# Other PSUM banks for the attention steps, and later places for one pair's V sums and for weight conversions

## The chip, the cores and the metric

The kernel runs on one core of a Trainium2 chip. The metric is the device time of one execution in microseconds. Before the change three runs took 580.83 us in the median (580.19 to 583.82).

Five engines work side by side, each with its own queue in order: TensorE (PE), VectorE (DVE), ScalarE (ACT), GpSimd (POOL) and SyncE (SP, which issues nearly all DMAs). PE writes its results to PSUM, which has eight banks of 2 KB in each of 128 partitions.

## The reference

Three layers follow each other, for a batch of 2, 768 positions and 8 heads of 64:

```
scores_l = scale * q @ k.T                      # only |i - j| < 16 counts
k_sum, v_sum = max of k, mean of v, over blocks of 32 positions
scores_s = scale * q @ k_sum.T + log(32)        # 24 block columns
a = softmax(concat(scores_l masked, scores_s))
x = a @ concat(v, v_sum)                        # attention, then heads side by side: 768 x 512

h = relu(x.T @ w_tok1) @ w_tok2                 # token mixing
u = x + h.T
x2 = u + relu(u @ w_ch1) @ w_ch2                # channel mixing, 512 -> 1536 -> 512

xn = layer_norm(x2) * g_ln
out = x2 + relu(xn @ w1) @ w2                   # 512 -> 2048 -> 512
```

## The kernel before, in words

**The attention part.** The heads are taken in pairs: two heads fill 128 partitions, and eight pairs, 0 to 7, make up both batches. A pair has twelve windows of 64 queries. A step handles four windows of a pair, so there are 24 steps, and step n belongs to pair n // 3. The keys of a window are 96 neighbours and the 24 block columns, 120 in all.

A step goes through six functions. `att_qk` (L378) makes the scores: 16 small matmuls into PSUM. `att_exp` (L398) has DVE add the mask and take the extreme of each row (L409, four instructions), and ACT take the exponential (L419, four instructions). `att_tr` (L421) transposes the four blocks of probabilities on PE into one bank of the pool `ps_pt`. `att_evac` (L429) has ACT copy that bank to SBUF (L433). `att_av` (L435) multiplies with V: 16 matmuls into one bank of the pool `ps_av`. `att_norm` (L454) has DVE divide by the row sums (L460, L463) into `u`.

**The preparation of a pair.** `prep_k` (L326, DVE) and `copy_k` (L339, ACT) make the block maxima of K. `prep_v1` (L345) makes the block sums of V: on DVE for pair 0, on POOL for the other pairs (L358, L361), from the transposed copy VT. `prep_v2` (L363) transposes these sums on PE (L367), into a bank of the same pool `ps_pt`, and ACT copies them into V in two instructions (L369). Q, K and V have three buffers each, VT and Z (the sums) two.

**PSUM banks.** The pool `ps_mm` has two banks for everything else. The scores are one tile of two banks: its axes are the window's parity j (one bank each), the step's parity, and the window couple. So two successive steps stand in two halves of the same two banks. `ps_pt` and `ps_av` have two banks each. Dependencies within a PSUM tile are kept bank by bank: an instruction of PE that writes a bank waits for the readers of that bank. A pool with n buffers hands a bank out again when all who used it are done.

**Weights.** The weights come as 64-bit words and are rebuilt as fp32 in halves of 512 columns. `conversion` (L160) is a generator of small pieces. For the first halves, four pieces make up one half: a load of a later half (`load_half`, L184, on SP, three buffers), one ACT instruction (L133) and three DVE instructions (L150, L152, L156), and the split into a rounded part (ACT, L203) and a rest (DVE, L228). During attention at most the first eight halves are done (L1107).

**Order of the work.** `attention` (L1019) writes out an order by hand: `put(at, ...)` enters a function at a place `at`, counted in steps, and the entries are sorted by place. PE keeps this order exactly. The other engines get theirs from a planner that goes by the same order and by its own estimate of when things are ready. The entries of step n are: scores at n, exponentials at n + 0.5, transposes at n + 1.1, the copy at n + 1.55, products at n + 2.15, and the normalisation at n + 2.6, with pieces of conversion woven in: `self.ops` pieces, which is 0 at the start, 4 from place 3.5 and 2 from place 8.58. Up to place 8.58 each step also has four matmuls on zeros, which keep PE busy (`fill`, L1070). The transpose of pair i's V sums stands at 3i - 0.2, ahead of the scores of step 3i at 3i and of the transposes of step 3i - 1 at 3i + 0.1; for pair 0 it stands at 1.6. From place 8.58 on, blocks of the token mixing are placed between the steps (`g1`, `g2`), and later the transposes for the channel mixing (`transpose_u`), at half steps or whole steps apart (L1049 to L1063).

**After attention** come the channel mixing, the layer norm and the last layer. PE's matmuls there run in an order set by loops in `run` (L1090).

Of the kernel before, what the change touches and what calls it, by code (L numbers as in the profile page):

```python
# [10 lines left out]
F32 = mybir.dt.float32  # L11
# [8 lines left out]
PSUM = bass.MemoryType.PSUM  # L20
DRAM = bass.MemoryType.DRAM

P = 128
# [37 lines left out]
class Kern:  # L61
# [316 lines left out]
    def att_qk(self, n):  # L378
        nc = self.nc
        i, qd = divmod(n, 3)  # L380
        Q, K = self.Q[i % 3], self.K[i % 3]
        ps = self.scores[:, :, n % 2]
        for e in range(2):
            for r in range(2):
                for j in range(2):
                    w = 4 * qd + 2 * e + j
                    a = 184 * (w // 2) + 88 * j
                    rows, cols = slice(64 * r, 64 * r + 64), slice(64 * (r ^ j), 64 * (r ^ j) + 64)
                    nc.tensor.matmul(  # L389
                        ps[cols, j, e, :NK],  # L390
                        Q[rows, 64 * w : 64 * w + 64],
                        K.rearrange("p v c -> p (v c)")[rows, a : a + NK],
                        start=True,
                        stop=True,
                    )
        self.sc[n] = ps
# [622 lines left out]
    def attention(self):  # L1019


        npair, nq = B * NPAIR, 3 * B * NPAIR
        O = ORDER
        ev = []
        put = lambda at, *fns: ev.append((at, len(ev), fns))
        for i in range(npair):
            at = 3 * i
            if i > 1:
                put(at + O["load_k"], lambda i=i: self.load_pair(i))
                put(at + O["load_vt"], lambda i=i: self.load_vt(i))  # L1030
                put(at + O["load_v"], lambda i=i: self.load_v(i))
            put(at + (O["kmax"] if i != 1 else -0.46), lambda i=i: self.prep_k(i))
            put(at + (O["copy_k"] if i != 1 else -0.44), lambda i=i: self.copy_k(i))
            put(at + O["vsum"] if i else O["vsum0"], lambda i=i: self.prep_v1(i))
            put(at + O["vput"] if i else O["vput0"], lambda i=i: self.prep_v2(i))
        for n in range(nq):
            put(n, lambda n=n: self.att_qk(n))
            if n < O["bg"]:
                put(n + 0.02, lambda: self.fill(2))
                put(n + 0.25, lambda: self.fill(2))  # L1040
            put(n + O["exp"], lambda n=n: self.att_exp(n))
            put(n + O["tr"], lambda n=n: self.att_tr(n))
            put(n + O["evac"], lambda n=n: self.att_evac(n))
            put(n + O["av"], lambda n=n: self.att_av(n))
            put(n + O["norm"], lambda n=n: self.weave(self.att_norm(n), self.convert(self.ops)))
        put(0.0, lambda: self.load_half(0), lambda: self.load_half(1))
        put(O["conv"], lambda: setattr(self, "ops", 4))
        put(O["bg"], lambda: setattr(self, "ops", 2))
        x0, x1, w0, w1 = self.g1(0, 0), self.g1(0, 1), self.g1(1, 0), self.g1(1, 1)  # L1049
        y, z0, z1 = self.g2(0), self.transpose_u(0), self.transpose_u(1)  # L1050
        low = {x0: 5 + O["lo"], x1: 11 + O["lo"], w0: 17 + O["lo"], w1: 23 + O["lo"]}
        need = {x0: 3, x1: 3, w0: 3, y: 6}
        pieces = [(x0, 0), (x0, 1), (x1, 0), (x1, 1)] + [(y, 1)] + [(y, 0.5)] * 5
        pieces += [(w0, 1), (w0, 0.5)] + [(z0, 0.5)] * 4 + [(z1, 0.5)] * 4 + [(w1, 0.5), (w1, 0.5)]
        at = O["bg"]
        for k, (g, gap) in enumerate(pieces):
            at += gap
            while at < low.get(g, 0):
                at += 0.5
            if g in need:  # L1060
                put(at, lambda g=g: self.convert_until(need[g]))
            put(at, lambda g=g: self.begin(g))
            put(at + O["fin"], lambda g=g: self.end(g))  # L1063
        for _, _, fns in sorted(ev, key=lambda e: e[:2]):
            for fn in fns:
                fn()
        while self.evacs:
            self.end(self.evacs[0])
# [21 lines left out]
    def run(self):  # L1090
        tc, nc, ctx = self.tc, self.nc, self.ctx
# [22 lines left out]
        xctx, actx = ExitStack(), ExitStack()  # L1114
# [1 line left out]
        self.att = actx.enter_context(tc.tile_pool(name="att", bufs=1, side="right"))  # L1116
        self.ps_mm = ctx.enter_context(tc.tile_pool(name="ps_mm", bufs=2, space=PSUM))
        ps_sc = actx.enter_context(tc.tile_pool(name="ps_sc", bufs=1, space=PSUM))
        self.scores = ps_sc.tile([P, 2, 2, 2, P], F32, name="scores")
        self.ps_pt = actx.enter_context(tc.tile_pool(name="ps_pt", bufs=2, space=PSUM))  # L1120
        self.ps_av = actx.enter_context(tc.tile_pool(name="ps_av", bufs=2, space=PSUM))

        att = self.att
        self.Q = [att.tile([P, S], F32, name=f"Q{i}") for i in range(3)]
# [67 lines left out]
        for n, (s, f, g) in enumerate(units):  # L1192
            if n == 0:
                order.enter_context(tc.manual_schedule(engines={mybir.EngineType.Activation}))
            c = 3 + f
# [28 lines left out]
            if xctx is not None and not self.bg and not self.evacs:  # L1224
# [7 lines left out]
                at = lambda f: self.slot(3 + f)  # L1232
# [130 lines left out]
```

## Time and profile before

| What | Value |
| --- | --- |
| Median of three runs | 580.83 us |
| Profiled execution | 580.95 us |
| Its span, first to last instruction | 579.2 us |
| PE busy | 561.1 us (97%) |
| DVE busy | 424.2 us (73%) |
| ACT busy | 296.8 us (51%) |
| POOL busy | 23.1 us (4%) |
| Mean granted clock of PE | 0.994 |

An engine is counted as busy while it executes, not while it waits. The shares are means over parts of the kernel with different limits, so the part that a change touches has to be read for itself. The granted clock is a share of PE's full speed: 1.00 is the level of 2.4 GHz, 0.50 that of 1.2 GHz.

### The profile page before, as it was taken

The page shows a single profiled execution, that of the slowest core. Times are in us where ns is not written, and L with a number is a line of the kernel's source. Part 1 is how long each engine was busy: PE and PEld are TensorE (multiplying, and loading weights), DVE is VectorE, ACT ScalarE, POOL GpSimd, SP SyncE. Part 2 cuts the span into 40 slices and gives each one's busy share as a digit, 9 for nine tenths or more (in the row PEclk, how much of TensorE's full clock was granted, in tenths as well). Part 3 has the DMA queues.
Part 4 walks back from the last instruction along what each step waited for, and adds up shares of the span by engine and source line. Part 5 has one row for each costly group of instructions (what it writes and reads, how often), then busy time and mean ns, then how long its engine had stood idle before and what let it go on. Part 6 is the DMA issues. An engine that isn't in the chain of part 4 may idle for free.

```text
span 579.2 us, 10262 instructions
## 1 busy us (share of the span) xinstructions
PE 561.1 (97%) x3651; PEld 494.7 (85%) x3656; DVE 424.2 (73%) x1012; ACT 296.8 (51%) x629; POOL 23.1 (4%) x54
## 2 busy tenths in 40 slices
PE   8798998999999999999999999999999999999997
PEld 3466776889998889999988988888898999999997
DVE  4598966576887689756659989686875986677781
ACT  4598757326875654755578455454331232233320
POOL 0424400000000000000000000000000000000000
PEclk9799999999999999999999999999999999999999
DMA  8999910133658766788936898786989998777545
GB/s 276 337 301 304 276 62 2 38 109 110 227 209 277 252 225 231 272 307 294 321 117 240 273 334 295 267 287 230 339 270 308 317 316 291 240 226 233 185 147 181
DMA packets 61417, 137.88 MB, mean 238 GB/s; under 512 B 5811, under 2 KB 19891, under 8 KB 61366
## 3 DMA queue, kind: packets, MB, share of 16 engines
q1 hardware_dynamic: 61360, 137.21, 71.8%
q8 instruction: 29, 0.48, 0.3%
q14 instruction: 22, 0.18, 0.1%
q10 hardware_dynamic: 6, 0.02, 0.0%
HBM read 102.60 MB, written 34.60 MB: 237 GB/s over the span
## 4 chain that ended last, share of the span: by engine, by line
PE 75%; DVE 10%; DMA 6%; ACT 5%; issue 2%; POOL 0%; SPq 0%; ACTq 0%; DVEq 0%; POOLq 0%
PE m L302 6%; PE m L304 5%; PE m L303 5%; PE acc_x L303 2%; PE acc_x L304 2%; PE acc_x L302 2%; PE g L475 2%; PE acc_y L304 2%; PE acc_y L303 2%; PE acc_y L302 2%; DMA VT<-in_vt_dram 1%; ACT pr L419 1%; PE av L446 1%; DMA w2s<-sp 1%; DMA wr<-w2s 1%
## 5 line engine op out<-in xcount | busy, mean ns | idle before, releaser
L302 PE MATMUL m<-slot,slot 128*128 128x384 f32 (+1 forms) x141 | 47.6, 338 | 1.9 <-DVE um L769 1.6
L304 PE MATMUL m<-slot,slot 128*128 128x384 f32 (+1 forms) x141 | 46.8, 332 | 0.0
L303 PE MATMUL m<-slot,slot 128*128 128x384 f32 (+1 forms) x141 | 46.8, 332 | 0.0
L303 PE MATMUL acc_x<-slot,ah 128*128 128x512 f32 x96 | 37.8, 394 | 0.0
L304 PE MATMUL acc_x<-slot,al 128*128 128x512 f32 x96 | 37.8, 394 | 0.0
L302 PE MATMUL acc_x<-slot,ah 128*128 128x512 f32 x96 | 37.5, 391 | 0.0
L419 ACT ACTIVATE pr<-sn,mn 128x120 f32<-128x120 f32 x96 | 30.2, 384 | 11.9 <-DVE mn L409 11.8
L302 PEld LDWEIGHTS m<-slot,slot 128*128 128x128 f32 x141 | 26.5, 188 | 5.4 <-DVE um L769 2.9
L303 PEld LDWEIGHTS m<-slot,slot 128*128 128x128 f32 x141 | 26.5, 188 | 1.5
L409 DVE CUSTOM_DVE_ANT_0 sn<-scores,mask 128x120 f32<-128x120 f32 x96 | 21.4, 277 | 8.3 <-PE scores L389 8.0
L304 PEld LDWEIGHTS m<-slot,slot 128*128 128x128 f32 x141 | 26.5, 188 | 0.0
L152 DVE SCALAR_TENSOR_TENSOR dec<-stage,dec 128x512 uint32<-128x512 uint32 x36 | 25.2, 700 | 0.5
L156 DVE SCALAR_TENSOR_TENSOR dec<-stage,dec 128x512 uint32<-128x512 uint32 x36 | 24.7, 687 | 0.4
L133 ACT ACTIVATE dec<-stage 128x512 f32<-128x512 f32 x36 | 24.2, 674 | 0.0
L760 ACT ACTIVATE ah<-sm 128x384 fp32r<-128x384 f32 x16 | 8.4, 526 | 30.7 <-DVE sm L769 30.7
L158 DVE SCALAR_TENSOR_TENSOR dec<-stage,dec 128x512 uint32<-128x512 uint32 x23 | 15.9, 690 | 9.5 <-ACT stage L139 9.3
L475 PE MATMUL g<-u,tok 128*128 128x256 f32 x96 | 22.5, 386 | 0.0
L304 PEld LDWEIGHTS acc_x<-slot,al 128*128 128x128 f32 x96 | 18.0, 188 | 4.0
L136 ACT ACTIVATE dec<-stage 128x512 f16<-128x512 f32 x23 | 18.4, 799 | 4.0 <-DMA stage<-in_wts_dram 4.0
L475 PEld LDWEIGHTS g<-u,tok 128*128 128x128 f32 x96 | 17.7, 190 | 2.9 <-issue 0.5
L358 POOL TENSOR_TENSOR VT<-VT 128x384 f32<-128x384 f32 (+3 forms) x28 | 18.3, 654 | 48.8 <-DMA VT<-in_vt_dram 47.1
L304 PE MATMUL acc_y<-slot,al_s 128*128 128x256 f32 x72 | 20.1, 280 | 0.0
(1492 smaller groups left out, 1760.1 us busy)
## 6 DMA issues: line engine op xcount, KB each, us to landing
stage<-in_wts_dram SPq DMA_DIRECT2D x62, 512.0 KB, 4.5
slot<-w1s SPq DMA_DIRECT2D x94, 256.0 KB, 4.1
w1s<-sps SPq DMA_DIRECT2D x16, 512.0 KB, 4.0
w2s<-sp SPq DMA_DIRECT2D x16, 512.0 KB, 3.0
slot<-w2s SPq DMA_DIRECT2D x16, 512.0 KB, 4.5
w2t<-wk SPq DMA_DIRECT2D x16, 512.0 KB, 4.7
slot<-w2t SPq DMA_DIRECT2D x8, 768.0 KB, 6.9
slot<-w2s SPq DMA_DIRECT2D x22, 256.0 KB, 4.3
```

Source lines behind the costliest of these rows:

```text
L133: nc.scalar.activation(m, high, AF.Abs, scale=2.0**-112)
L136: nc.scalar.activation(q[:, :, 1].bitcast(F16), high, AF.Copy, scale=2.0**-60)
L152: put(m, t[:, :, 1], 0x80000000, m, op0=ALU.bitwise_and, op1=ALU.bitwise_or)
L156: put(m, t[:, :, 0], 29, m, op0=ALU.logical_shift_right, op1=ALU.bitwise_or)
L158: put(m, t[:, :, 1], 3, m, op0=ALU.logical_shift_left, op1=ALU.bitwise_or)
L302: nc.tensor.matmul(out, lhs[0], rhs[0], start=first, stop=False)
L303: nc.tensor.matmul(out, lhs[0], rhs[1], start=False, stop=False)
L304: nc.tensor.matmul(out, lhs[1], rhs[0], start=False, stop=last)
L358: nc.gpsimd.tensor_tensor(cur[:, :, 0:n], cur[:, :, 0:n], cur[:, :, n : 2 * n], op=ALU.add)
L409: self.ttr[n] = nc.vector.tensor_tensor_reduce(sn[:, u], ps[:, u % 2, u // 2, :NK], self.mask[:, mv], scale=-SCALE, scalar=3e38, op0=ALU.a ...
L419: nc.scalar.activation(pr[:, u], sn[:, u], AF.Exp, bias=mn[:, u : u + 1], scale=-1.0)
L475: nc.tensor.matmul(ps[:, :256], self.tok1(st, t), self.u[:, b * ST + st, 256 * hf : 256 * hf + 256], start=st == 0, stop=st == ST - 1,)
```

## The change

- The scores become two tiles of two banks each. Step n uses tile n % 2; within it, window parity j still has a bank of its own. So the scores have four banks instead of two.
- `ps_pt` and `ps_av` get one bank each instead of two. All eight banks are in use before and after.
- The transpose of the V sums of pair 1, with its copies, moves from place 2.8 (3 - 0.2) to place 4.6 (3 + 1.6). Pair 0 and pairs 2 to 7 keep their places.
- `self.ops` is 0 from place 8.58, 4 from place 10.9 and 2 from place 16.9; before it was 2 from place 8.58 on.

```diff
@@ att_qk
-        ps = self.scores[:, :, n % 2]
+        ps = self.scores[n % 2][:, :, 0:256].rearrange("p j (e c) -> p j e c", e=2)
@@ attention
-            put(at + O["vput"] if i else O["vput0"], lambda i=i: self.prep_v2(i))
+            put(at + O["vput"] if i > 1 else at + O["vput0"], lambda i=i: self.prep_v2(i))
@@
-        put(O["bg"], lambda: setattr(self, "ops", 2))
+        for at, n in ((O["bg"], 0), (10.9, 4), (16.9, 2)):
+            put(at, lambda n=n: setattr(self, "ops", n))
@@ run
-        self.scores = ps_sc.tile([P, 2, 2, 2, P], F32, name="scores")
-        self.ps_pt = actx.enter_context(tc.tile_pool(name="ps_pt", bufs=2, space=PSUM))
-        self.ps_av = actx.enter_context(tc.tile_pool(name="ps_av", bufs=2, space=PSUM))
+        self.scores = [ps_sc.tile([P, 2, 512], F32, name=f"scores{i}") for i in range(2)]
+        self.ps_pt = actx.enter_context(tc.tile_pool(name="ps_pt", bufs=1, space=PSUM))
+        self.ps_av = actx.enter_context(tc.tile_pool(name="ps_av", bufs=1, space=PSUM))
```

## Rows read from the trace of the kernel before

**Rows 1.** Part 2 of the page: DMA share in 40 slices, in tenths.
```profile
DMA  8999910133658766788936898786989998777545
```
**Rows 2.** Table of stretches: length, busy us (instructions) per engine, clock, DMA, GB/s.
```profile
18.00:24.00 6.00, 5.25 (x52) 3.28 (x57) 3.12 (x13) 4.59 (x9) 0.36 (x2) 0.52 1.07 344
...
28.00:56.00 28.00, 25.47 (x355) 18.04 (x361) 25.01 (x114) 25.88 (x63) 9.55 (x18) 1.00 1.04 303
56.00:88.00 32.00, 31.95 (x334) 24.83 (x325) 23.99 (x94) 20.04 (x52) 6.58 (x13) 1.00 0.58 174
88.00:101.00 13.00, 11.23 (x173) 8.55 (x172) 8.82 (x41) 10.85 (x27) 0.00 (x0) 1.00 0.01 2
101.00:579.00 478.00, 470.90 (x2606) 431.97 (x2604) 352.51 (x706) 225.35 (x454) 0.00 (x0) 1.00 0.72 241
```
**Rows 3.** Timeline of PE: start us, us, instruction, [idle before <- releaser]; pair 1's V sums.
```profile
18.42 0.47 PE L367 MATMUL psv<-ident,Z 128*120 128x128 f32 x1 [3.39 <-POOL Z L361]
```
**Rows 4.** PE's waits, 6 to 101 us: who waited for whom, us, times, longest.
```profile
PE psv L367 <- POOL Z L361: 3.4, 1, 3.4
PE tu L518 <- DVE xt L523: 1.7, 1, 1.7
PE av L446 <- ACT PT L433: 1.0, 3, 0.5
PE scores L389 <- DVE mn L409: 1.0, 2, 0.6
```
**Rows 5.** Timeline around the V sums of pair 2, engine by engine.
```profile
24.30 3.04 POOL L358 TENSOR_TENSOR VT<-VT 128x384 f32<-128x384 f32 x4 [5.94 <-DMA VT<-in_vt_dram]
...
27.42 0.41 POOL L361 TENSOR_TENSOR Z<-VT 128x24 f32<-128x24 f32 x2
...
28.98 0.27 PE L367 MATMUL psv<-ident,Z 128*120 128x128 f32 x1
...
30.20 0.70 PE L426 MATMUL pt<-ident,pr 128*120 128x128 f32 x4
...
30.42 1.61 ACT L369 ACTIVATE V<-psv 24x768 f32<-24x768 f32 x2
```
**Rows 6.** Timeline around the V sums of pair 3.
```profile
40.32 0.27 PE L367 MATMUL psv<-ident,Z 128*120 128x128 f32 x1
...
41.09 0.65 PE L426 MATMUL pt<-ident,pr 128*120 128x128 f32 x4
...
40.80 1.61 ACT L369 ACTIVATE V<-psv 24x768 f32<-24x768 f32 x2
```
**Rows 7.** Timeline of steps 8 to 13, around the V sums of pair 4.
```profile
47.54 0.64 PE L389 MATMUL scores<-K,Q 64*64 64x120 f32 x16 [0.62 <-DVE mn L409]
...
49.24 0.69 PE L446 MATMUL av<-V,PT 121*64 121x65 f32 x16 [0.48 <-ACT PT L433]
49.86 0.33 PE L367 MATMUL psv<-ident,Z 128*120 128x128 f32 x1
...
50.90 1.10 PE L426 MATMUL pt<-ident,pr 128*120 128x128 f32 x4
...
53.60 1.18 PE L426 MATMUL pt<-ident,pr 128*120 128x128 f32 x4 [0.42 <-ACT pr L419]
...
48.67 0.41 DVE L463 TENSOR_TENSOR u<-av,rec 128x256 f32<-128x256 f32 x1
...
51.51 1.61 ACT L369 ACTIVATE V<-psv 24x768 f32<-24x768 f32 x2
```
**Rows 8.** Timeline around the V sums of pair 7.
```profile
88.94 1.62 ACT L369 ACTIVATE V<-psv 24x768 f32<-24x768 f32 x2
...
89.62 0.60 PE L426 MATMUL pt<-ident,pr 128*120 128x128 f32 x4
```
**Rows 9.** Groups by line, 28 to 64 us: busy us, mean ns, then idle before.
```profile
L152 DVE SCALAR_TENSOR_TENSOR dec<-stage,dec 128x512 uint32<-128x512 uint32 x6 | 4.5, 750 | 0.1
...
L228 DVE TENSOR_TENSOR slot<-dec,slot 128x512 fp32r<-128x512 f32 x5 | 3.8, 785 | 0.0
```

## The prediction

> **What bounds the kernel now.** I read the page's slices first, to see where anything but TensorE (PE) can set the time. The DMA row is full for the first five of forty slices, about 72 us, and nearly empty for the next two [rows 1]: those are the loads of the attention part. A table of stretches then splits the span [rows 2]. From 101 us to the end PE is busy 470.90 of 478 us, and that is work the change does not touch. From 56 to 88 us PE is busy 31.95 of 32: the attention steps there carry blocks of the token mixing, and PE sets the pace. From 28 to 56 us three engines are close together: PE 25.47, ACT 25.88, DVE 25.01 of 28 us. So ACT alone would need 25.88 us there whatever PE waits for. From 88 to 101 us PE idles 1.77 us. So all that the change can win lies ahead of 101 us.
>
> Third, the waits and the timeline of PE. The longest wait is for the V sums of pair 1: the transpose of those sums begins at 18.42 us, after PE has stood still 3.39 us for GpSimd (POOL) [rows 3]. The granted clock in 18 to 24 us is 0.52, the level of 1.2 GHz; in the other stretches shown it is 1.00 [rows 2]. In the list of PE's waits the score banks are small: 1.0 us in two waits, against 3.4 for the V sums, 1.7 for the x transposes and 1.0 for the probabilities' copy [rows 4].
>
> **V sums of pair 1 placed later.** Moved past on PE: the scores of steps 3 and 4, transposes of steps 2 and 3, products of steps 1 and 2; on ACT its two copies into V fall behind the exponentials of steps 3 and 4. It issues no DMA. Gross it frees 3.39 us, and if the clock stays up, half of the 5.25 busy us of 18 to 24 us, 2.6 more [rows 2, 3]. But the next transpose of this kind, pair 2's, needs POOL's sums of pair 2, and these end at 27.83 (27.42 + 0.41), because POOL sat 5.94 us waiting for that pair's VT, which the full DMA row delivers [rows 1, 5]. PE reached it at 28.98. Freed of both costs PE would be there at 28.98 - 3.39 - 2.6 = 23.0, plus about 2 us for the two waits with one bank (pair 0's sums behind the copy of step 0, pair 1's V copies): near 25, and it then stands until 27.83. So what is kept is 28.98 - 27.83 = **1.15 us**, between 0 and 1.15; the wait has moved one pair on. Will this wait pull the clock down as the old one did? At worst another 2.6 us. The only drop followed 3.39 us without work; the 1.7 us wait at the x transposes left its stretch at 1.00 [rows 2, 4]. About 2.8 us lies between them, and I take 0.
>
> **Four score banks.** Scores of step n+1 no longer wait until DVE has read step n. Two waits, 1.0 us together, go [rows 4]; 0.62 of it is at step 11 (47.54 us) [rows 7], the rest ahead of 28 us, where the wait for pair 2 swallows it. Worth **0.6**, bounds 0 and 1.0.
>
> **One bank for transposed probabilities.** Two prices. First, the transposes of step n must wait until ACT has copied step n-1 out. Today only the product behind them waits, three times, 1.0 us in all [rows 4]. At those three places four transposes (about 0.53 us) come behind the wait instead of under it: 0 to 1.6 us. I take 0.3, since ACT is the engine that is late, and the delay also lets it catch up. Second, the V sums use the same bank. PE issues pair i's transpose, then scores, then the probabilities of step 3i-1; these now stand until both V copies (1.61 us) are through ACT. In the trace the copies start 0.48 us after the transpose of pair 3 (40.32), but 1.44 after pair 2's and 1.65 after pair 4's (49.86), where ACT had a queue. With 0.48 they end 2.09 us after it. Next to where the transposes start today that makes 28.98 + 2.09 - 30.20 = 0.87 for pair 2, 42.41 - 41.09 = 1.32 for pair 3, 51.95 - 50.90 = 1.05 for pair 4 and 90.55 - 89.62 = 0.93 for pair 7 [rows 5 to 8]: 4.2 us. In today's order of ACT it is 1.83 + 1.32 + 2.22 + 0.93 = 6.3. For pairs 5 and 6 a block of token mixing stands between and covers it; without that cover they would cost as much as pair 3.
>
> What of it reaches the end? Pair 4: the transposes of steps 11 and 12 already crawl today, 1.10 and 1.18 us instead of about 0.6, with 0.42 idle between, because their exponentials come late [rows 7]. That is 1.5 us of waiting for the same ACT; the new 1.05 takes its place, net -0.3 with part of the product's wait behind it. Pair 7: behind it PE waits 1.7 us for the x transposes' evacuation on ACT and DVE [rows 4]; 0.93 earlier shortens that one: 0. Pair 2: 0.87 less the 0.28 that the product of step 5 waits today: +0.6. Pair 3: 1.32, less the 0.62 at step 11 (counted above, so here not again) and the 0.48 at the product of step 9 [rows 7]: +0.8.
>
> The row shows only three waits for that copy in 24 steps [rows 4]. The Trainium skill (Perfetto Trace Analysis, section Matmuls) says that independent groups on PE should rotate through different PSUM banks so that evacuation of one overlaps the next; it speaks for the score banks and against the other two. Were it to hold at every step, the slower rival below would be the case.
>
> **One bank for products.** The next product must wait for DVE's normalisation. The tightest place is step 8's, which ends at 49.08, 0.16 us ahead of the product of step 9, itself waiting for ACT [rows 7]. 0, at most 0.5; the cover is that DVE keeps normalisations in step order.
>
> **Conversions later.** Between 8.58 and 10.9 none are interleaved, then four per step instead of two. By step 14 both orders have issued 32 such pieces, so neither DVE nor ACT has more to do in total. SP's loads of the next halves move with them, behind the loads of pairs 4 and 5; with three buffers filled ahead they cost nothing, else up to a wait. Four pieces are one half, and of a half's four DVE instructions two take 0.75 and 0.79 us [rows 9]; taking all four so, a half is near 3 us, and the steps from 11 on carry 1.5 us more each. Two of them lie ahead of the next block of token mixing (place 14.08): 0 to 3 us. I take 0, as DVE has 3.0 us free in 28 to 56 us [rows 2].
>
> **Sum.** -1.15 - 0.6 + 0.3 - 0.3 + 0 + 0.6 + 0.8 = -0.35. The profiled execution took 580.95 us (span 579.2, 1.75 around it), 0.12 above the median of 580.83. Forecast **580.6 us**.
>
> **Rivals.** *Faster*: ACT orders its copies so well that PE never stands. The limit is 1.15 + 2.1 (ACT's free time in 28 to 56 us) + 1.77 (88 to 101 us) = 5.0 [rows 2], or 575.9; more only if conversions slip past 56 us, where ACT has room. For it: PE's idle time there is all waiting. Against: ACT is 92% busy.
> *Slower*: one mechanism, PE standing at the probabilities' transposes behind ACT because the bank is single. At today's order of ACT, 6.3 + 1.6 - 1.15 - 0.6 = +6.2, or 587.1. It decides once the copies start over 1.4 us after their transpose, as they do at pairs 2 and 4; against it, half of that is taken from waits that exist.
> *No effect*: the order on DVE and ACT is planned ahead, and ready conversions may be drawn forward into the gap, with the waits merely exchanged: 581. *Clock*: the new wait at pair 2 drops it: +2.6, or 583.
>
> **Numbers.** Forecast with no effect and clock (578 to 583) 0.62; faster rival (under 578) 0.16, about half of it under 575.0; slower rival (over 583) 0.22, somewhat over half of it above 586.8. A change of this kernel under 1%, 5.8 us, is told from nothing only with difficulty, and that is the bound here: faster 0.08, same 0.79, slower 0.13. Range 576 to 586: the lower end is the faster rival's limit, the upper stops short of the slower rival at full price and leaves out about 2 in 10 in all.
>
> **What would show it.** In the profile after: pair 1's wait for POOL gone from PE, a wait for POOL at pair 2 of 2 to 3 us with scores of step 6 near 28 us; the score waits gone; new waits of PE's transposes for V copies, near 1 us at pairs 2, 3, 4 and 7; the attention part's end near 101 us within 2 us of before, and nothing new behind it. Wrong if VT of pair 2 lands far from 24.3 us, if these waits are 2 us or more, or if the work behind 101 us changes length.

## The result, and the profile after

After the change the median of eleven runs is **587.71 us** (583.31 to 590.35), against 582.00 (580.19 to 584.93) for eleven runs of the kernel before: a ratio of **1.0089 [1.0070, 1.0108]**, so the change costs 0.9%. Forecast were 580.6 us and a range of 576 to 586. The price that the text gave its slower rival, 587.1, lies 0.6 us from the result; that sum starts from 580.95, and the runs beside the change had 582.00, so the rival's +6.2 us stands against +5.7 measured.

The profiled execution after took 590.35 us, the longest of the eleven, with a span of 588.6 us and a granted clock of 0.986. First its summary, part 1 and the clock's row of part 2.

```profile
PE 565.8 (96%) x3656; PEld 496.5 (84%) x3656; DVE 424.5 (72%) x1012; ACT 298.4 (51%) x629; POOL 22.2 (4%) x54
...
PEclk9879899999999999999999999999999999999999
```

Two numbers split the loss of this execution. PE's idle time is span less busy time: 588.6 - 565.8 = 22.8 us, before 579.2 - 561.1 = 18.1. So 4.7 of the 9.4 us of span are standing still, and 4.7 are longer busy time for the same matmuls. The second half is the clock: taken from the mean granted clocks, 565.8 x 0.014 - 561.1 x 0.006 = 7.9 - 3.4 = 4.5 us, an estimate.

The table of stretches shows where; its columns are those of [rows 2].

```profile
18.00:24.00 6.00, 6.00 (x81) 3.62 (x80) 5.03 (x25) 4.47 (x12) 0.00 (x0) 0.89 1.07 328
28.00:56.00 28.00, 22.82 (x255) 15.56 (x254) 19.93 (x79) 19.99 (x47) 10.08 (x22) 0.88 0.87 267
56.00:88.00 32.00, 29.95 (x338) 22.87 (x335) 24.67 (x98) 22.54 (x55) 6.60 (x12) 0.95 0.67 215
88.00:101.00 13.00, 11.61 (x138) 9.02 (x136) 6.41 (x35) 8.67 (x22) 0.00 (x0) 1.00 0.01 1
```

From 18 to 24 us PE now works without a gap, 6.00 of 6 us for 5.25, at a clock of 0.89 for 0.52: the wait for POOL and the fall behind it are gone from there (another fall ends in it, see below). But from 28 to 56 us PE, ACT and DVE are all less busy than in [rows 2] (22.82 for 25.47, 19.99 for 25.88, 19.93 for 25.01): none of the three fills the stretch. Part of their work has moved behind it (255 matmuls of PE for 355), since PE is late. The clock there is 0.88, and 0.95 in the next stretch; both were 1.00.

PE's waits from 6 to 112 us, who waited for whom, us, times, longest:

```profile
PE pt L426 <- ACT V L369: 6.7, 6, 1.7
PE psv L367 <- ACT PT L433: 5.6, 4, 3.3
PE tu L518 <- DVE xt L523: 0.6, 1, 0.6
PE av L446 <- DVE u L463: 0.4, 1, 0.4
```

Against [rows 4], the waits for POOL and for the score banks have left the list, as the prediction said, and so have those of the products for L433. In their place stand 12.3 us at the single bank of transposed probabilities, in two directions: the probabilities wait until ACT has copied the V sums out of it (6.7), and the V sums wait until ACT has copied the probabilities out (5.6). The second kind the prediction had named for pair 0 alone, and there under a cover. The x transposes' wait is shorter, 0.6 for 1.7.

The timeline of PE at these places (start, length, instruction, idle before and releaser) shows pairs 0 to 4 in order:

```profile
11.54 0.30 PE L367 MATMUL psv<-ident,Z 128*120 128x128 f32 x1 [1.80 <-ACT PT L433]
...
14.86 1.11 PE L426 MATMUL pt<-ident,pr 128*120 128x128 f32 x4 [1.64 <-ACT V L369]
...
24.36 0.29 PE L367 MATMUL psv<-ident,Z 128*120 128x128 f32 x1 [0.33 <-ACT PT L433]
...
26.38 0.65 PE L426 MATMUL pt<-ident,pr 128*120 128x128 f32 x4 [0.61 <-ACT V L369]
...
31.45 0.30 PE L367 MATMUL psv<-ident,Z 128*120 128x128 f32 x1 [3.27 <-ACT PT L433]
...
33.47 1.11 PE L426 MATMUL pt<-ident,pr 128*120 128x128 f32 x4 [0.61 <-ACT V L369]
...
48.06 0.65 PE L426 MATMUL pt<-ident,pr 128*120 128x128 f32 x4 [1.30 <-ACT V L369]
...
58.81 0.65 PE L426 MATMUL pt<-ident,pr 128*120 128x128 f32 x4 [1.70 <-ACT V L369]
```

Pair 2's V sums begin at 31.45, where before it was 28.98 [rows 5]. What held them is on ACT, in the same view:

```profile
26.59 0.39 ACT L419 ACTIVATE pr<-sn,mn 128x120 f32<-128x120 f32 x1
29.18 0.66 ACT L133 ACTIVATE tok<-stage 128x512 f32<-128x512 f32 x1 [2.20 <-DMA stage<-in_wts_dram]
29.75 0.95 ACT L419 ACTIVATE pr<-sn,mn 128x120 f32<-128x120 f32 x3
30.72 0.59 ACT L433 COPY PT<-pt 120x512 f32<-120x512 f32 x1
31.79 1.63 ACT L369 ACTIVATE V<-psv 24x768 f32<-24x768 f32 x2 [0.48 <-PE psv L367]
```

Read from the bottom: the V sums had to wait for the copy of the probabilities at 30.72, this stood in ACT's queue behind three exponentials, and these behind a weight conversion (L133) whose words had not landed: 2.20 us of ACT standing still for a DMA. With two banks the V sums would not have had to wait for that copy.

POOL had these sums ready a little earlier, and not at the 27.83 of [rows 5]:

```profile
26.11 2.49 POOL L358 TENSOR_TENSOR VT<-VT 128x384 f32<-128x384 f32 x4 [8.86 <-DMA VT<-in_vt_dram]
28.68 0.41 POOL L361 TENSOR_TENSOR Z<-VT 128x24 f32<-128x24 f32 x2
```

They were there at 29.09. So in this execution the transfer of VT alone took the forecast gain away (29.09 is later than 28.98), and the wait at the single bank added 31.45 - 29.09 = 2.36 us there.

The clock in windows of 4 us (same columns as the stretches):

```profile
12.00:16.00 4.00, 2.36 (x24) 1.09 (x18) 1.72 (x9) 3.02 (x7) 1.59 (x2) 0.57 1.06 294
16.00:20.00 4.00, 4.00 (x40) 2.31 (x40) 1.88 (x12) 2.02 (x5) 1.07 (x4) 0.58 1.06 372
...
28.00:32.00 4.00, 0.73 (x14) 0.46 (x17) 2.09 (x5) 2.31 (x6) 0.94 (x4) 1.00 1.05 319
32.00:36.00 4.00, 3.39 (x38) 1.98 (x28) 1.18 (x10) 3.24 (x7) 1.29 (x2) 0.63 1.05 295
36.00:40.00 4.00, 4.00 (x38) 2.35 (x38) 2.09 (x10) 1.42 (x5) 1.36 (x5) 0.52 1.04 362
...
60.00:64.00 4.00, 4.00 (x57) 2.98 (x54) 2.82 (x14) 3.89 (x10) 0.00 (x0) 0.57 0.65 233
```

Three times PE falls to the level of 1.2 GHz, each time behind a wait at that bank. In windows of 1 us the clock is 0.76 in 12 to 13 us, behind the wait of 1.80 us at pair 0 and still ahead of the one of 1.64; it is 0.50 in 33 to 34, behind the 3.27 at pair 2, and 0.66 in 60 to 61, behind the 1.70 at pair 4. Behind the 1.30 at pair 3 it stays at 1.00. Before there was one fall, in the wait of 3.39 us. After the second fall the first block of token mixing starts at 43.33 where it started at 37.73, 5.6 us late; at 31.68 the scores of step 6 had been 2.5 us late (29.18 before). The first matmul of the channel mixing is 8.0 us late (114.03 for 106.07).

### The profile page after: what moved, and what is told of

Same layout as the page of the kernel before. It is cut to its first block, busy times and chain, and to the rows that moved or that the text cites. A ratio compares the mean times of both kernels' runs of the same rounds, so it can differ in the third digit from the quotient of the medians.

```text
span 588.6 us, 10276 instructions
## 1 busy us (share of the span) xinstructions
PE 565.8 (96%) x3656; PEld 496.5 (84%) x3656; DVE 424.5 (72%) x1012; ACT 298.4 (51%) x629; POOL 22.2 (4%) x54
## 4 chain that ended last, share of the span: by engine, by line
PE 71%; DMA 11%; DVE 9%; ACT 6%; issue 2%; SPq 0%; ACTq 0%; DVEq 0%
PE m L302 6%; PE m L304 5%; PE m L303 5%; PE g L475 4%; DMA stage<-in_wts_dram 3%; DMA V<-in_v_dram 2%; PE acc_x L303 2%; PE acc_x L304 2%; PE acc_x L302 2%; PE acc_y L304 2%; PE acc_y L303 2%; PE acc_y L302 2%; PE av L446 2%; PE pt L426 2%; DMA w1s<-sps 2%
## 5 line engine op out<-in xcount | busy, mean ns | idle before, releaser
L419 ACT ACTIVATE pr<-sn,mn 128x120 f32<-128x120 f32 x96 | 30.6, 385 | 12.3 <-DVE mn L409 12.1
L409 DVE CUSTOM_DVE_ANT_0 sn<-scores,mask 128x120 f32<-128x120 f32 x96 | 21.6, 277 | 3.9 <-PE scores L389 3.7
L133 ACT ACTIVATE dec<-stage 128x512 f32<-128x512 f32 x36 | 24.3, 676 | 0.1
L426 PE MATMUL pt<-ident,pr 128*120 128x128 f32 x96 | 17.2, 304 | 6.7 <-ACT V L369 6.7
L426 PEld LDWEIGHTS pt<-ident,pr 128*120 128x120 f32 x96 | 12.3, 150 | 12.4 <-ACT V L369 9.1
```

The lines of the kernel that those rows point to most:

```text
L133: nc.scalar.activation(m, high, AF.Abs, scale=2.0**-112)
L409: self.ttr[n] = nc.vector.tensor_tensor_reduce(sn[:, u], ps[:, u % 2, u // 2, :NK], self.mask[:, mv], scale=-SCALE, scalar=3e38, op0=ALU.a ...
L419: nc.scalar.activation(pr[:, u], sn[:, u], AF.Exp, bias=mn[:, u : u + 1], scale=-1.0)
L426: nc.tensor.transpose(ps[:NK, u * P : u * P + P], pr[:, u], self.ident)
```

## The experiments

Theory (S in the expectations): PE stands behind ACT at the single bank of transposed probabilities, and that alone is the loss. Rivals: the two moved places cost it (V sums of pair 1, D; conversions, C); the clock's falls cost it (K); and Q, as some expectations call it: the conversion words that ACT waits for set the early part whatever the banks are, so that their place in the order decides.

All ratios are to the kernel before on the same chip, in five rounds. PE's idle time is span less busy time of the profiled execution (18.1 us before).

| Kernel | Median, before | Ratio | Span, PE idle, clock |
| --- | --- | --- | --- |
| pt1_only | 587.54, 581.85 | 1.0106 [1.0080, 1.0133] | 584.0, 23.2, 0.994 |
| av1_only | 583.37, 583.29 | 1.0003 [0.9980, 1.0027] | 581.2, 20.2, 0.994 |
| banks_only | 586.17, 582.01 | 1.0085 [1.0064, 1.0105] | 585.2, 21.0, 0.985 |
| vput_only | 583.19, 581.85 | 1.0019 [1.0000, 1.0037] | 579.3, 19.1, 0.997 |
| conv_only | 581.04, 581.85 | 0.9987 [0.9968, 1.0005] | 578.6, 18.3, 0.994 |
| places_only | 581.62, 582.68 | 1.0001 [0.9978, 1.0024] | 579.6, 18.8, 0.997 |
| psv_mm_only | 584.80, 582.68 | 1.0046 [1.0025, 1.0066] | 581.9, 21.5, 0.997 |
| pt1_psv_mm | 586.83, 582.68 | 1.0080 [1.0055, 1.0104] | 583.1, 22.1, 0.994 |
| psv_av_only | 581.97, 582.00 | 0.9998 [0.9976, 1.0020] | 581.5, 19.2, 0.994 |
| pt1_psv_av | 585.13, 582.00 | 1.0051 [1.0022, 1.0080] | 584.4, 21.2, 0.990 |
| after_psv_mm | 585.12, 581.85 | 1.0064 [1.0038, 1.0089] | 581.8, 21.1, 0.993 |
| after_psv_av | 589.11, 582.00 | 1.0122 [1.0086, 1.0157] | 587.9, 23.4, 0.988 |
| after_fills | 593.93, 582.01 | 1.0201 [1.0177, 1.0225] | 593.0, 24.0, 0.988 |
| vput_conv45 | 583.02, 582.01 | 1.0015 [0.9997, 1.0032] | 581.0, 19.7, 0.994 |
| pt1_conv45 | 588.34, 582.01 | 1.0117 [1.0097, 1.0138] | 585.9, 25.8, 0.993 |
| vput_late_loads | 585.69, 583.29 | 1.0047 [1.0028, 1.0066] | 584.7, 20.4, 0.991 |
| after_late_loads | 585.98, 583.29 | 1.0050 [1.0029, 1.0071] | 583.2, 20.3, 0.991 |
| after_psv_mm_late | 586.89, 583.29 | 1.0084 [1.0046, 1.0122] | 585.4, 23.8, 0.993 |

### The parts of the change, one at a time

**pt1_only**: the kernel before, with one bank for transposed probabilities.

```diff
-        self.ps_pt = ... tile_pool(name="ps_pt", bufs=2, space=PSUM))
+        self.ps_pt = ... tile_pool(name="ps_pt", bufs=1, space=PSUM))
```

> The kernel before with one change: the pool for transposed probabilities has one bank instead of two (seven banks in use). Theory S (the single bank makes PE stand behind ACT, and the clock falls in those waits): 585 to 588 us, 4 to 6 above before; PE's transposes wait for V copies at five or six places and the transposes of V sums wait for the copy of the probabilities, together 6 us or more. Rival D (the loss comes from data that lands late, once V sums of pair 1 no longer hold PE): within 1 us of before. Rival C (the conversions bunched at steps 11 to 16 cost it): within 1 us of before.

Measured 1.0106: one number changed in the source brings a loss as large as the change's. Its waits of PE, 6 to 112 us, one more from the list behind 100 us, and its stretch from 28 to 56 us:

```profile
PE pt L426 <- ACT V L369: 5.8, 6, 1.3
PE psv L367 <- ACT PT L433: 4.8, 4, 1.9
PE pt L426 <- ACT PT L433: 1.3, 2, 0.7
...
PE tu L518 <- DVE al_('u', 0)_14_2343 L640: 1.3, 1, 1.3
```

```profile
28.00:56.00 28.00, 21.05 (x282) 15.06 (x285) 23.87 (x92) 23.64 (x56) 9.34 (x17) 1.00 1.02 312
```

The 11.9 us of the first three lines replace waits of [rows 4], above all the 3.4 for POOL, which no longer shows because PE comes to pair 1's sums late anyway (18.34 against 18.42). PE's idle time grows by 23.2 - 18.1 = 5.1 us, the span by 4.8. Its profiled clock is 0.994 as before, so in that execution the loss is waiting alone. That run, 585.80 us, is the fastest of six; the other five have clocks of 0.982 to 0.991 and take up to 588.66, and the median holds them. In the stretch where [rows 2] had three engines at 25 to 26 of 28 us, all three are now idler: PE 21.05, DVE 23.87, ACT 23.64.

Where does PE fall behind? Its V sums of pairs 1, 2, 3, 4 and 7 begin at 18.34, 29.94, 41.59, 53.14 and 91.47, against 18.42, 28.98, 40.32, 49.86 and 88.47 before, and the channel mixing at 109.04 against 106.07. So 1.0 us is lost between pairs 1 and 2, 0.3 up to pair 3, 2.0 up to pair 4, and nothing more up to the channel mixing, where it is 3.0. The other 1.8 us of the span come behind the attention part. There the last wait of the list is new: 1.3 us at x transposes near 200 us, for a DVE instruction (L640) that stood behind pieces of conversion. From the channel mixing to the end the four kernels whose names begin with `pt1` take 474.2 to 476.2 us in their profiles, the kernel before 473.1 and the others 471.9 to 474.6. Why these four are at the upper end stays open.

**av1_only**: the kernel before, with `bufs=1` for `ps_av`.

> The kernel before with only one bank for the products with V instead of two (seven banks in use). Theory S: within 1 us of before, since the next product hardly ever waits for the normalisation. Rival A: 583.5 or more, with waits of the products for DVE of 2 us or more in all.

The single bank of products costs nothing that can be told.

**banks_only**: the change without the two moved places, that is the diff of `att_qk` and of `run` alone.

> The changed kernel with only its banks: four for the scores, one each for transposed probabilities and products; V sums of pair 1 and conversions at their old places. Theory S (the one bank for transposed probabilities is the whole loss, the score banks win next to nothing): 586 to 588 us, as with that one bank alone (587.5). Rival B (the score banks win what they were meant to win): 583 to 585, 3 or more below that kernel. Rival A (the single bank for products costs something too): 589 or more.

1.0085, against 1.0106 for one of these banks alone: the score banks and the products' bank together give back 0.2 points, but the intervals overlap, so it may be nothing. In its profile all of the loss lies ahead of the channel mixing, which starts at 112.05, 6.0 us late.

**vput_only**: the kernel before, with the first line of the diff of `attention`.

> The kernel before with only the V sums of pair 1 moved from place 2.8 to 4.6. Theory S: with two banks PE runs on until POOL's sums of pair 2 hold it; 579 to 582 us, 0 to 2 below before, and no long stretch at half clock. Rival D: PE then stands for conversion data or for pair 2's sums as long as it stood before, or longer: 582 to 585.

The wait for POOL at pair 1 went, and others came. ACT from 16 to 24 us, DVE's first piece of the same conversions, and PE's scores of step 4:

```profile
18.09 0.66 ACT L133 ACTIVATE tok<-stage 128x512 f32<-128x512 f32 x1 [2.70 <-DMA stage<-in_wts_dram]
20.52 0.68 ACT L133 ACTIVATE tok<-stage 128x512 f32<-128x512 f32 x1 [1.77 <-DMA stage<-in_wts_dram]
21.11 1.23 ACT L419 ACTIVATE pr<-sn,mn 128x120 f32<-128x120 f32 x4
```

```profile
18.78 0.43 DVE L150 TENSOR_SCALAR tok<-tok 128x512 uint32<-128x512 uint32 x1 [4.26 <-ACT tok L133]
...
20.80 0.94 PE L389 MATMUL scores<-K,Q 64*64 64x120 f32 x16 [2.59 <-DVE mn L409]
```

Before, those two conversions began at 20.57 and 22.89 without a wait: the 3.39 us of [rows 3] had also been the time in which their words landed. Freed of it, ACT and DVE come too early for the words. On DVE the masks of step 3 (L409, 19.85 us) stand behind L150, though their scores were done at 16.08; the scores of step 4 wait for these masks, and pair 2's sums begin at 28.82, 0.16 us earlier than before, not 1.15. So for this kernel rival D of its expectation was right (583.19 us, in its 582 to 585); as the cause of the change's loss D falls with pt1_only and places_only.

**conv_only**: the kernel before, with the conversions' places of the change.

> The kernel before with only the conversions placed later (none from place 8.58, four per step from 10.9, two from 16.9). Theory S: within 1 us of before. Rival C: 584 to 587, with new waits of PE for exponentials or copies between 50 and 62 us.

**places_only**: both moved places, the banks as before.

> The two moved places of the change together (V sums of pair 1 at 4.6, conversions 0, 4, 2), the banks as before. If the parts add, 1.0019 - 0.0013 gives a ratio of 1.0006 and the whole loss of the change is the banks'. If the two places collide over ACT and DVE, above 1.003; the prediction's sum without its bank terms would be -1.15 us, a ratio of 0.998.

0.9987 and 1.0001: the places cost nothing. With banks_only the parts add up: 1.0085 and 1.0001 against 1.0089. The first rival falls.

### Who pays at the single bank

The V sums share the bank with the probabilities. Moving only their transposes to another pool splits the price; each move needs its control with two banks.

```diff
-        ps = self.ps_pt.tile([P, 512], F32, tag="pt", name=f"psv{i}")
+        ps = self.ps_mm.tile([P, 512], F32, tag="mm", name=f"psv{i}")   # psv_mm_only, pt1_psv_mm, after_psv_mm
+        ps = self.ps_av.tile([P, 512], F32, tag="av", name=f"psv{i}")   # psv_av_only, pt1_psv_av, after_psv_av
```

Each name says which kernel the line stands in: `_only` the kernel before, `pt1_` that of pt1_only, `after_` the change.

> The changed kernel, but the transpose of the V sums takes a bank of the two-bank pool ps_mm, so that it shares no bank with the probabilities. Theory S: the waits of PE's transposes for V copies (6.7 us) and of the V sums' transposes for the probabilities' copy (5.6 us) go; 578 to 582 us, 5 to 8 below the changed kernel, granted clock 0.993 or more. Rival D: PE stands for late data instead, within 2 us of the changed kernel. Rival C: within 2 us of the changed kernel.

> The control: two banks of transposed probabilities as before, only the V sums' transposes go to the pool of two banks. If that move is free, ratio 0.999 to 1.001 and POOL's wait at pair 1 stays near 3.4 us; if the V sums there collide with the token mixing, which uses the same pool, the ratio is above 1.002 and that share of pt1_psv_mm's loss is not the single bank's.

> The kernel before with one bank of transposed probabilities, and the V sums' transposes in the pool of two banks instead of that bank. If the loss is PE standing behind the V copies (5.8 us of waits in pt1_only), this gives most of it back: ratio to before at most 1.004, and the wait of the transposes for L369 is gone with no new one above 2 us. If the probabilities' own copy behind ACT's queue is the larger price, the wait turns into one for L433 of 3 us or more and the ratio stays above 1.007. Equal shares would give about 1.005.

> The control: banks as before, only the V sums' transposes stand in the two banks of the products with V. If the V copies there are hidden, as DVE's normalisation frees the other bank early, ratio 0.999 to 1.002; if products then wait for the V copies (1.61 us), above 1.003.

> One bank for transposed probabilities, V sums in the two banks of the products. If the sharing of one bank with the V copies is most of pt1_only's 1.0106, this gives at most 1.004 with no wait of transposes for L369; if the probabilities' own copy is half of it or more, at least 1.005 with waits for L433 of 3 us or more. From the split in the general banks (1.008 less the 1.0046 of its control) I expect 1.0034.

> The whole change, with the V sums' transposes in the single bank of the products. If the four score banks are worth the 0.6 us of the prediction and the V sums were the loss, 1.002 or less; if single banks cost whichever of the two the V sums share, 1.006 to 1.009 as in the change itself, now with products waiting for the V copies.

In the change, the move into the general pool gives 1.0064 for 1.0089, with intervals that overlap and 3 us above what the theory expected, and the wait changes its name:

```profile
PE pt L426 <- ACT PT L433: 6.5, 6, 2.9
```

In the general pool the move is not free: its control takes 1.0046, with the token mixing waiting 2.4 us for the V copies. So of the 1.0080 of pt1_psv_mm about 1.0034 is the single bank's, if the two add. In the products' pool the move is free: 0.9998. So that pair of kernels is the clean one. With one bank for the probabilities and the V sums elsewhere the ratio is 1.0051; PE's longest waits in pt1_psv_av:

```profile
PE psv L367 <- POOL Z L361: 3.9, 2, 3.0
PE pt L426 <- ACT PT L433: 2.4, 3, 1.1
```

So the bank that the probabilities have to themselves costs 0.0051 x 582.0 = 3.0 us [1.3, 4.7], and sharing it with the V sums the rest of pt1_only's 0.0106 x 581.85 = 6.2, about 3.2 us; from the two intervals 0.9 to 5.5. About half and half is what was measured, though neither share is sharp, and the result lies between the two conditions of the expectation (1.0051, but 2.4 us of waits for 3). These are times of the whole kernel and not waits at the bank: in the profiles the channel mixing starts at 108.24 in pt1_psv_av and at 107.68 in its control, only 0.6 us apart, and the rest comes behind it, where PE waits 2.4 us for L640 (control 0.8). So the price in time is measured, and the way it comes about is not. after_psv_av tries the V sums in the change's single bank of products: it takes 1.0122, above the 1.006 to 1.009 expected, PE's V sums now waiting 4.7 us for DVE's normalisation (L463), and the probabilities 4.1 us for L433. So a bank that cost nothing with one user (1.0003) brings waits with two; that the time is above the change's 1.0089 is not shown, the intervals overlap.

### The clock

**after_fills**: the change, with matmuls on zeros ahead of the three long waits.

```diff
+        for at, n in ((1.58, 8), (2.08, 7), (5.78, 14)):
+            put(at, lambda n=n: self.fill(n))
```

> The changed kernel with 29 more matmuls on zeros just ahead of three of PE's new waits: 8 ahead of the transpose of pair 0's V sums, 7 ahead of the transposes of step 1, 14 ahead of the transpose of pair 2's V sums; each group is shorter than the wait that it fills. Theory K (a good part of the loss is the half clock that follows the waits): 583 to 585 us, 3 to 5 below the changed kernel, and no stretch below 0.9 of the clock ahead of 40 us. Rival W (the waits alone make the loss): within 1.5 us of the changed kernel.

This failed as a test. The time rose by 6 us more, to 1.0201, outside both expectations, since the waits moved. The longest, 3.23 us, now stands at 21.24 us at the transposes, for a copy (L433) that ACT began only after two conversions whose words it had waited for. The fourteen matmuls ran from 33.10 to 38.0 us, with hardly a wait left to fill (POOL's sums were ready at 29.22, and the copy that frees the bank ended at 33.75), partly at the half clock, and the clock still fell (0.50 in 20 to 24 us, 0.67 in 32 to 36). What the clock costs apart from the waits that precede it is not shown by an experiment. Two profiles come near it. pt1_only and banks_only wait about as long at the bank, 11.9 and 10.9 us; the clock falls once in pt1_only, in 12 to 20 us, and in banks_only also in 28 to 36 (0.82 and 0.75) and 52 to 64 (0.81, 0.50 and 0.84); the channel mixing starts 3.0 and 6.0 us late. So two falls go with about 3 us, an estimate from one execution of each. What is shown besides are the eleven runs of the change, which have the same instructions: the ones at 0.994 and 0.991 took 583.31 and 584.07 us, the nine at 0.985 to 0.988 took 587.38 to 590.35.

### The order of the conversions

**vput_conv45** and **pt1_conv45**: vput_only and pt1_only, with the conversions woven in from place 4.5, not 3.5.

```diff
-"conv": 3.5
+"conv": 4.5
```

> The kernel before with the V sums of pair 1 at place 4.6 and the conversions' start at 4.5 instead of 3.5; banks as before. Theory Q (with pair 1's V sums out of the way, ACT's queue stood at the first conversions, whose words had not landed, and DVE and PE behind it): PE's 2.6 us wait for scores of step 4 goes; then PE is held by POOL's sums of pair 2 at 28 us at the latest, and the time is 579.5 to 581.5, 1 to 3 below the version with the old start. Rival R (the waits are only exchanged): 582.5 to 584, with another wait of 2 us or more ahead of 28 us.

> The kernel before with one bank for transposed probabilities and the conversions' start at 4.5 instead of 3.5. Theory S1 (the single bank costs through the V copies and the probabilities' copy wherever ACT is late): 586 to 588 us, as without the later start. Rival Q1 (it costs because the copy stands behind conversions whose data have not landed): 582 to 584.

The edit did not do what it was to do: the first two conversions still stand ahead of the exponentials of step 3 on ACT (the first waits 2.72 us for its words in vput_conv45), since the planner draws them forward. 1.0015 and 1.0117 are the ratios of vput_only and pt1_only again, within their intervals, and say nothing on Q.

**vput_late_loads**, **after_late_loads** and **after_psv_mm_late**: vput_only, the change and after_psv_mm, with the conversions from place 5.5 and the first two loads later too.

```diff
-        put(0.0, lambda: self.load_half(0), lambda: self.load_half(1))
+        put(1.5, lambda: self.load_half(0), lambda: self.load_half(1))
-"conv": 3.5
+"conv": 5.5
```

> The kernel before, banks as before, with the V sums of pair 1 at place 4.6, the first two conversion loads at place 1.5 instead of 0 (SP then issues them behind pair 2's loads) and the conversions' start at 5.5, so that in ACT's and DVE's queues the first conversion words stand behind the exponentials of steps 3 to 5. Theory Q (with the V sums out of the way, ACT and DVE stood at conversion words whose data had not landed, and PE behind them): no wait of PE above 1.5 us between 14 and 28 us, POOL's sums of pair 2 earlier by 2 us or more, and 578 to 580.5 us, 2 to 4 below before. Rival R (the time is set behind 28 us by ACT and DVE, whatever PE gains ahead of it): 581 to 583, a lead at step 6 that is gone by step 14.

> The changed kernel with the same two shifts (first conversion loads at place 1.5, conversions from 5.5). Theory S2 (the single bank for transposed probabilities costs wherever ACT is late, and ACT is late for more reasons than conversion data): still 585 to 588 us. Rival Q2 (the single bank costs mainly because the copies stand behind conversion words that wait for data): 581 to 583.

> The changed kernel with V sums' transposes in the pool ps_mm and the same two shifts of the conversions. If both causes add up (V copies in the same bank, and copies of the probabilities behind conversion words): 580 to 582.5 us, and PE's waits of probabilities' transposes for the copy before fall from 6.5 to under 3 us. If the single bank costs by itself, whatever delays ACT: 584 to 586.

Early on Q holds. In vput_late_loads pair 2's sums begin at 25.00 us, 3.98 us earlier than before. Then the lead is spent: the transposes at 35.71 wait 2.63 us for exponentials behind a conversion on ACT (L133, 34.71), which itself waited 3.17 us for its words. The first block of token mixing, which needs these words, starts at 37.96 (37.73 before) and the third at 59.60 (56.25). The time, 1.0047, is above both expectations. With this order the banks cost nothing further: after_late_loads takes 1.0050, less than the change's 1.0089 (the intervals just touch), though their waits are in its profile (7.0 us for L369, 3.3 for L433). So what a wait at the bank costs depends on what else stands in the queues, and that the bank alone makes the loss is shown for the old order of the conversions only. How the two combine, and why after_psv_mm_late is not below after_psv_mm, stays open. No version beats the kernel before by more than its interval.

## Why the prediction was wrong

**V sums of pair 1, -1.15 us: not there.** The mechanism was right in part: the wait at pair 1 went. But it had covered not one late transfer, but two: POOL's VT, which the text named, and the first conversion words, which it did not. vput_only gives -0.16 us at pair 2 and 1.0019 in time. The cap at 27.83 also took a landing time of one execution as fixed; after the change VT was ready at 26.11, not 24.30.

**Four score banks, -0.6: not contradicted.** The waits for L409 are gone from the list. banks_only against pt1_only allows about -1.2 us (2.1 thousandths of 582), and the intervals leave room for none.

**One bank for transposed probabilities, +1.4 net (0.3 + 0.6 + 0.8 - 0.3): measured +6.2 [4.7, 7.7]. This is the step that failed**, in the sentences under "What of it reaches the end?". What the text did price came out near: at the four pairs that it priced the V copies hold PE for 4.4 us after the change and 3.9 in pt1_only, for 4.2 to 6.3 (pair 3: 1.30 in both, 1.32 forecast; pair 4: 1.70 and 1.15, 1.05 forecast; pair 7: 0.83, 0.93 forecast). In pt1_only the subtraction of existing waits held too: from pair 4's V sums to the third block of token mixing PE takes 6.19 us for 6.39, as "net -0.3" said, and at pair 7 the wait at the x transposes fell from 1.7 to 0.6. After the change it did not hold at pair 4 (7.60 for 6.39, at the half clock behind the wait).

What failed is what the sum left out. First, the other direction: V sums that wait for the probabilities' copy. The text named it for pair 0 alone, under the cover of pair 1's wait, where pt1_only confirms it, and priced it at no other pair. It measured 1.90 us at pair 2 and 0.78 at pair 4 in pt1_only (4.8 in all with pair 0), and 5.6 after the change. Second, the copy's own price was put at 0.3 of a bound of 1.6: the waits for it are 1.3 us in pt1_only, and pt1_psv_av gives 3.0 in time. In the profile of pt1_only PE is 3.0 us late at the channel mixing, where these terms of the sum make 1.4. Third, the clock was put at 0 and the work behind 101 us at no change: up to 6.2 the rest is 1.8 us behind the channel mixing in this profile, and 1.4 that this trace does not hold. The other runs have lower clocks, and banks_only, with the same waits and two more falls, is 6.0 us late there.

**The list of waits.** The text had weighed three waits for the copy in 24 steps against the slower rival [rows 4]; those were the waits with two banks, and a list of waits says nothing of what a second bank has been hiding. The Trainium skill (Perfetto Trace Analysis, section Matmuls) says that independent groups on PE should rotate through different PSUM banks. The trace agrees for the probabilities, with 5.8 and 4.8 us of waits where one bank is left; for the products one bank cost nothing (1.0003).

**One bank for products, 0: right** (1.0003). **Conversions later, 0: right** (0.9987 alone).

**The clock at pair 2, 0: wrong in the profiled execution.** The wait there was 3.27 us, close to the 3.39 of [rows 3], and the same fall followed. The text's bound was 2.6 us for one fall; three came, two of them behind waits of 1.80 and 1.70 us, and the estimate above is 4.5 us more than before.

**Behind 101 us, nothing: not quite.** After the change the channel mixing starts 8.0 us late and the span ends 9.4 us later; 0.8 of the other 1.4 shows as new waits of PE (0.6 for L640 at the x transposes, 0.2 at the channel mixing). In pt1_only it is 1.8 of 4.8.

The rival "slower" had the mechanism, the place and, at 6.2 us, the price of pt1_only, though not its parts: its sum still held the -1.15 and left out the V sums behind the copy. Its condition, copies that start over 1.4 us after their transpose, was not met at most pairs: after the change they start 1.65 us behind it at pair 0 (13.19 for 11.54), but 0.34 at pairs 1 and 2, 0.48 at pair 3 and 0.90 at pair 4. So that 587.1 came so near is in good part luck. Of the signs that the text asked for, three came (no POOL wait at pair 1, no score waits, V-copy waits near 1 us); the POOL wait at pair 2 came as one for L433 with the scores of step 6 at 31.68 instead of near 28, one wait was over 2 us, and the attention part did not end within 2 us of before.

## What to carry to other kernels

A bank count that shows no waits may be what keeps them away: before taking a buffer from a pool, list every user of it in PE's order, and price both directions, writer behind reader for each pair of neighbours. Take a wait's price with what may follow it: here falls of the clock, and in pt1_only 1.8 of 4.8 us behind the stage. And a wait that is removed uncovers all that was landing meanwhile, so look at each queue's next transfer, not at the releaser's alone.

## What was not expected of the hardware

ACT takes its queue in order, also when its head waits for a DMA. After the change a conversion of 0.66 us stood 2.20 us for its words, and behind it three exponentials whose inputs DVE had finished at 26.34 us and the copy of a bank that PE had filled at 27.03. In vput_only such a stop of 2.70 us held DVE's masks too: DVE stood idle for 4.26 us. And the granted clock differs from run to run of one kernel: after the change it goes with 4 to 7 us (583.31 at 0.994, 587.38 to 590.35 at 0.985 to 0.988), in 25 runs of the kernel before with about 2 (579.54 to 582.16 in six at 0.997, 582.87 and 582.88 in two at 0.988; the 17 between them 579.60 to 583.79).
